# Ten small memsets in place of seven between two indirect writes

## The chip, the cores and the metric

One core of a Trainium2 chip runs the whole program in one launch. The metric is the device time of that launch in microseconds (us), the median of several executions; smaller is better. Before the change three executions took 780.31, 781.12 and 782.70 us, so the median is 781.12 us.

## The reference, cut to what matters

The program is sliding-window attention followed by a mixture of experts that drops no token (float32 throughout). Attention has 8 batches, 8 heads, 576 positions and a head size of 64; heads 0 to 3 look at the last 32 positions, heads 4 to 7 at every fourth of the last 128. The attention output becomes 4,608 token rows of 512 numbers. Each token goes to the one of 8 experts with the largest logit:

```python
scores = np.where(masks, SCALE * q @ k.T, -1e9)
attn   = softmax(scores)              # rows of 576
x      = (attn @ v) as (4608, 512)
logits = x @ w_gate                   # (4608, 8)
e      = argmax(logits, axis=1); gate = softmax(logits)[e]
for each expert: y = relu(x_e @ w1[e]) @ w2[e]    # 512 -> 1024 -> 512
out    = gate[:, None] * y            # back in token order
```

## The kernel before, in words

**Attention.** The 8 batches are cut into 32 units of work, four per batch. A unit goes through the engines in a fixed chain: scores on PE (line 595), masking and the row minimum on DVE (lines 611, 623), nine exponentials on ACT (line 629), the reciprocal of the sums on DVE (lines 640, 642), the normalisation on POOL (line 646, called the norm below), transposes on PE (line 657), their copies on ACT or DVE (line 878) and the product with V on PE (line 676). A ring of three buffers, `e`, holds units between masking and transposes.

**Routing.** After a batch's four units, `route` computes its logits, counts on DVE how many tokens each expert has so far, and writes the batch's 576 rows into a DRAM table called `bucket`, sorted by expert. It does so with five indirect DMAs issued by POOL (`to_bucket`, line 493). After the batches 1, 2, 4 and 7 DVE also computes tables of slots: a slot is 128 rows of one expert. The last route adds two indirect writes of blank rows.

**Experts.** A slot's rows are fetched from `bucket` by SP (`fetch_x`, lines 1379 and 1384), its weights by SP (line 1401), DVE transposes the rows (line 1407), PE does the two layers (lines 1415 and 1431), ACT applies relu and the gate, and POOL scatters the 128 result rows to their tokens by an indirect DMA (line 1456). Thirty such slots and fourteen short ones of 32 rows (lines 1518 to 1545, `own` and `toq` in the trace) are in the planned part. Three slots more come behind it under run-time conditions (`rest`). Slots after batch 1 are computed between the attention units of later batches.

**The order of the work.** No order is written by hand. Each piece of work is given to a planner (`Plan.add`) as a step, with its engines, a cost in us, the steps that it comes after, the buffers that it takes and a rank. `Plan.write` then builds the program: again and again it asks of every open step when it could start on each engine (`could`), takes the earliest time found, and of the steps that could start within 0.25 us of it emits the one of lowest rank. The instructions of each engine are emitted in that order and run in it. While PE is planned to be idle before the first slot, `Plan.write` emits filling matmuls (line 714) whose result nobody reads.

**Indirect writes in the plan.** POOL is planned at 1.0 us per indirect write. If the step that POOL did last was an indirect write too, `could` lets the next one start no earlier than `APART` after the end of the last one, and `write` has `pass_time` (line 720) emit `IDLE` memsets of one element per partition to the tile `still` ahead of it. Any other POOL step between two writes, such as a norm, clears that flag, and then there are no memsets. The planner counts one such memset at 0.21 us:

```python
APART = 0.21 * IDLE                                        # line 138
if s.moved and e == "POOL" and self.last_indirect:         # line 200
    at = max(at, self.wrote + self.APART)
if s.moved and e == "POOL" and self.last_indirect and self.APART:   # line 239
    self.idle()
```

Two further planner constants touch this: an indirect write that starts less than `BURST` (1.0 us) after the last one opens a stretch in which other engines' results are planned to be seen late (`seen`, lines 174 to 180).

Of the kernel before, what the change touches and what calls it, by code (L numbers as in the profile page):

```python
# [63 lines left out]
STEP_W = 1.0  # L64
ROUTE = 5.0

IDLE = 7

MOVED = 3.0
MOVED_S = 1.5  # L70
# [47 lines left out]
class Plan:  # L118
# [18 lines left out]

    APART = 0.21 * IDLE

# [189 lines left out]
def kernel(  # L329
# [390 lines left out]
    def pass_time():  # L720
        for _ in range(IDLE):
            nc.gpsimd.memset(still, 0.0)  # L722
# [1115 lines left out]
```

## Time and profile before

| | |
|---|---|
| runs (us) | 780.31, 781.12, 782.70 |
| profiled execution (us) | 781.74 |
| its span, first to last instruction (us) | 780.0 |
| mean granted TensorE clock | 0.991 |
| PE busy | 742.8 us, 95% of the span |
| DVE, ACT, POOL busy | 33%, 34%, 25% |
| memsets of line 722 | 504, in 72 groups of seven |

The rows come from the hardware profiler's record of that one execution. A row of a timeline has its start and its length in us, the engine, the line of the kernel, the operation, what it writes and reads, and how many instructions are merged in it; in brackets stands how long the engine sat idle before it and whose event ended the wait ("issue" is none that the profile shows). A row of a group of instructions has busy time and mean ns of one, and then the idle time ahead of them with its releasers. A row of a table of stretches has the busy time of each engine in that stretch.

### The profile page before, as it was taken

What the parts mean: (1) busy time and instruction counts of PE and PEld (TensorE: products, weight loads), DVE (VectorE), ACT (ScalarE), POOL (GpSimd) and SP (SyncE); (2) the same over time, 40 slices, a digit from 0 to 9 for tenths busy, and PEclk for the clock granted to TensorE, in tenths of its full rate; (3) what the DMA queues carried; (4) which work ended last, traced back from release to release, by engine and by line L of the source; (5) the groups of instructions that cost most, each with busy time, mean ns of one, the idle gap of its engine ahead of it and who ended that gap; (6) DMA issues with size and microseconds to landing.
All of it is one profiled execution on the core that took longest, in us unless ns stands there. A gap on an engine that the chain in (4) does not pass through costs nothing.

```text
span 780.0 us, 21889 instructions
## 1 busy us (share of the span) xinstructions
PE 742.8 (95%) x8406; PEld 562.4 (72%) x8406; DVE 257.6 (33%) x718; ACT 265.2 (34%) x868; POOL 193.5 (25%) x641
## 2 busy tenths in 40 slices
PE   5879989999999999999999999999999999999996
PEld 5768878868787776776776776777776776766664
DVE  7958858678857740710000000000000000000000
ACT  2766756576747754211111111111111111111100
POOL 1314343425253434260100100211221111102101
PEclk9989999999999999999999999999999999999999
DMA  9878775969997979799629684727678166099660
GB/s 274 301 224 272 229 239 137 361 190 323 260 268 178 298 226 350 262 387 323 214 47 314 201 258 100 254 51 250 196 261 299 35 226 261 22 316 351 257 222 30
DMA packets 140399, 180.68 MB, mean 232 GB/s; under 512 B 68764, under 2 KB 90014, under 8 KB 139776
## 3 DMA queue, kind: packets, MB, share of 16 engines
q1 hardware_dynamic: 132864, 159.00, 64.1%
q0 software_dynamic: 6272, 19.43, 6.5%
q8 instruction: 68, 1.11, 0.6%
q10 hardware_dynamic: 1152, 0.78, 0.4%
q14 instruction: 43, 0.35, 0.1%
HBM read 252.03 MB, written 19.95 MB: 349 GB/s over the span
## 4 chain that ended last, share of the span: by engine, by line
PE 80%; issue 8%; DMA 6%; DVE 3%; ACT 2%; POOL 1%; SPq 0%; POOLq 0%; DVEq 0%; ACTq 0%
PE ph L1415 27%; PE py L1431 25%; PE scores L595 6%; PE xo L676 6%; PE weights L657 4%; DMA qT<-in_moe_w_dram 4%; PE py_s L1545 3%; PE ph_s L1518 3%; PE weights L714 3%; PE xrow L939 2%; PE lp L962 1%; DMA raw<-in_k_dram 1%; DMA x<-bucket 1%; PE logits L976 1%; ACT eT L878 1%
## 5 line engine op out<-in xcount | busy, mean ns | idle before, releaser
L1415 PEld LDWEIGHTS ph<-xt,w 128*128 128x128 f32 x2112 | 243.2, 192 | 15.7 <-issue 14.6
L1415 PE MATMUL ph<-xt,w 128*128 128x128 f32 x2112 | 252.5, 277 | 0.0
L1431 PE MATMUL py<-w,h 128*128 128x512 f32 x528 | 236.5, 594 | 0.6 <-ACT h L1426 0.6
L1431 PEld LDWEIGHTS py<-w,h 128*128 128x128 f32 x528 | 96.0, 190 | 101.3 <-issue 100.8
L629 ACT ACTIVATE e<-e,lo 128x96 f32<-128x96 f32 x288 | 103.5, 363 | 19.6 <-DVE lo L623 19.6
L1407 DVE STREAM_TRANSPOSE xt<-x 128x512 f32<-128x512 f32 x30 | 21.3, 711 | 243.7 <-PE ph L1415 240.4
L1456 POOL DMA_INDIRECT out_dram<-y,to x30 | 29.5, 984 | 251.7 <-ACT y L1436 249.2
L646 POOL TENSOR_TENSOR e<-e,rec 128x864 f32<-128x864 f32 x32 | 52.3, 1633 | 141.1 <-DVE rec L642 112.6
L1426 ACT ACTIVATE h<-ph 128x512 f32<-128x512 f32 x63 | 37.6, 597 | 142.6 <-PE ph L1415 141.8
L1436 ACT ACTIVATE y<-py,gt 128x512 f32<-128x512 f32 x30 | 20.6, 687 | 157.8 <-PE py L1431 150.3
L595 PE MATMUL scores<-kT,qT 32*64 32x96 f32 (+1 forms) x2160 | 56.2, 259 | 12.0 <-issue 7.4
L595 PEld LDWEIGHTS scores<-kT,qT 32*64 32x64 f32 (+1 forms) x2160 | 49.1, 139 | 18.5 <-issue 14.3
L722 POOL MEMSET still<- 128x1 f32 x504 | 51.4, 102 | 25.0
L629 ACT ACTIVATION_READ_ACCUMULATOR e<-e,lo 128x1 f32 x288 | 54.4, 189 | 0.0
L493 POOL DMA_INDIRECT bucket<-rows,idx x40 | 39.2, 980 | 60.9 <-issue 16.9
L676 PEld LDWEIGHTS xo<-eT,v 96*64 96x64 f32 x1280 | 40.9, 138 | 12.3 <-issue 4.5
L657 PE MATMUL weights<-cst,e 128*96 128x128 f32 x288 | 45.1, 282 | 4.5 <-ACT eT L878 2.1
L611 DVE SCALAR_TENSOR_TENSOR e<-scores,cst 128x384 f32<-128x384 f32 (+1 forms) x128 | 45.5, 395 | 10.0 <-PE scores L595 9.0
L676 PE MATMUL xo<-eT,v 96*64 96x64 f32 (+1 forms) x1280 | 45.9, 225 | 3.0 <-issue 2.6
L878 ACT COPY eT<-weights 96x384 f32<-96x384 f32 x88 | 39.9, 480 | 22.8 <-PE weights L657 16.1
L657 PEld LDWEIGHTS weights<-cst,e 128*96 128x96 f32 x288 | 30.2, 129 | 17.2 <-issue 6.8
L1511 DVE STREAM_TRANSPOSE own<-own 128x128 f32<-128x128 f32 x14 | 4.3, 304 | 99.3 <-DMA own<-bucket 99.3
(168 smaller groups left out, 566.5 us busy)
## 6 DMA issues: line engine op xcount, KB each, us to landing
w<-in_moe_w_dram SPq DMA_DIRECT2D x66, 2048.0 KB
raw<-in_moe_w_dram SPq DMA_DIRECT2D x42, 1024.0 KB
qT<-in_moe_w_dram SPq DMA_DIRECT2D x28, 512.0 KB
w<-in_moe_w_dram SPq DMA_DIRECT2D x8, 1024.0 KB
raw<-in_q_dram SPq DMA_DIRECT2D x14, 576.0 KB
raw<-in_k_dram SPq DMA_DIRECT2D x14, 576.0 KB
x<-bucket SPq DMA_DIRECT2D x120, 64.0 KB
v<-in_v_dram SPq DMA_DIRECT2D x7, 864.0 KB
```

Source lines behind the costliest of these rows:

```text
L493: nc.gpsimd.indirect_dma_start(out=bucket, out_offset=bass.IndirectOffsetOnAxis(ap=idx, axis=0), in_=rows, in_offset=None, bounds_check=NR ...
L595: nc.tensor.matmul(two[r][QB * half : QB * half + QB, KB * c : KB * c + KB], lhsT=qT[:, QB * n : QB * n + QB], rhs=kt[:, QB * n : QB * n + ...
L611: nc.vector.scalar_tensor_tensor(out=e[p, c0 : c0 + w], in0=sc[r][p, a : a + w], scalar=-SCALE, in1=m[p, a : a + w], op0=OP.mult, op1=OP.add,)
L629: nc.scalar.activation(out=ev[:, c], in_=ev[:, c], func=AF.Exp, bias=lo[:, c : c + 1], scale=-1.0, accum_out=den[:, c : c + 1],)
L646: nc.gpsimd.tensor_tensor(out=ev, in0=ev, in1=rec.unsqueeze(2).broadcast_to([128, NC, KB]), op=OP.mult)
L657: nc.tensor.transpose(tp[0:KB, c], ev[:, 3 * g + c], ident)
L676: nc.tensor.matmul(xo[DH * r : DH * r + DH, g, lo - half_s * g : hi - half_s * g], lhsT=v0[:, hd, n] if ty == 0 else v1[:, n, hd], rhs=eT[ ...
L722: nc.gpsimd.memset(still, 0.0)
L878: copier(e)(S_["eT"][:, 3 * g : 3 * g + 3], S_["w", g][0:KB, 0:3])
L1415: nc.tensor.matmul(ph[:, f % 4], lhsT=w1s[j % 2][:, c, 128 * f : 128 * f + 128], rhs=xt[:, c], start=c == 0, stop=c == 3,)
L1426: nc.scalar.activation(to, ph, AF.Relu)
L1431: nc.tensor.matmul(py, lhsT=h[:, f], rhs=w2s[j % 2][:, f], start=f == 0, stop=f == 7)
```

## The change

One constant changes. `IDLE` enters in two places: in `pass_time`, which emits that many memsets, and in `APART`, which goes from 1.47 to 2.10 us.

```diff
-IDLE = 7
+IDLE = 10
```

## Rows read from the trace of the kernel before

**Rows 1.** The page: span and busy time of the engines.

```profile
span 780.0 us, 21889 instructions
...
PE 742.8 (95%) x8406; PEld 562.4 (72%) x8406; DVE 257.6 (33%) x718; ACT 265.2 (34%) x868; POOL 193.5 (25%) x641
```

**Rows 2.** Table of stretches: start and end, length, busy us of each engine (instructions), granted clock, DMA share, GB/s.

```profile
0.00:72.00 72.00, 56.49 (x1130) 49.85 (x1131) 55.30 (x117) 40.34 (x171) 17.34 (x30) 0.93 0.86 271
72.00:136.50 64.50, 59.21 (x1082) 51.87 (x1083) 49.37 (x139) 43.13 (x162) 25.10 (x56) 1.00 0.68 204
136.50:345.00 208.50, 200.96 (x2757) 157.70 (x2756) 127.35 (x383) 119.01 (x419) 83.19 (x249) 1.00 0.90 279
345.00:720.00 375.00, 373.65 (x3091) 267.42 (x3090) 22.84 (x77) 57.07 (x107) 62.23 (x296) 1.00 0.64 212
720.00:780.00 60.00, 52.45 (x352) 35.58 (x350) 2.69 (x4) 5.66 (x10) 5.60 (x12) 0.97 0.47 175
```

**Rows 3.** Groups of instructions on PE, from 72 to 136.5 us: the filling matmuls. Then one piece of the chain of work that ended last, in which 24 of them follow one another.

```profile
L714 PE MATMUL weights<-idle 128*128 128x128 f32 x130 | 17.6, 280 | 2.4 <-ACT eT L878 1.7 <-DVE eT L878 0.7
...
100.98 2.94 PE weights L714 x24
```

**Rows 4.** Groups of instructions on POOL: the memsets of line 722 from 72 to 345 us, then from 345 to 735 us, and in the latter stretch the scatters of results.

```profile
L722 POOL MEMSET still<- 128x1 f32 x231 | 23.6, 102 | 11.4
...
L722 POOL MEMSET still<- 128x1 f32 x266 | 27.1, 102 | 13.2
L1456 POOL DMA_INDIRECT out_dram<-y,to x25 | 24.5, 980 | 249.2 <-ACT y L1436 248.4 <-issue 0.7
L1456 POOL DMA_INDIRECT out_dram<-own,toq x14 | 13.7, 978 | 61.8 <-ACT own L1556 30.5 <-DVE toq L1562 18.4 <-DMA qT<-in_moe_w_dram 4.8
```

**Rows 5.** Timeline of POOL, around the first two routes.

```profile
70.76 1.05 POOL L722 MEMSET still<- 128x1 f32 x7
72.46 0.99 POOL L493 DMA_INDIRECT bucket<-rows,idx  x1 [0.65 <-issue]
73.43 1.07 POOL L722 MEMSET still<- 128x1 f32 x7
75.15 0.98 POOL L493 DMA_INDIRECT bucket<-rows,idx  x1 [0.65 <-issue]
...
78.84 1.65 POOL L646 TENSOR_TENSOR e<-e,rec 128x864 f32<-128x864 f32 x1
...
101.49 1.01 POOL L493 DMA_INDIRECT bucket<-rows,idx  x1 [8.97 <-DVE avail L1182]
...
110.55 1.65 POOL L646 TENSOR_TENSOR e<-e,rec 128x864 f32<-128x864 f32 x1
112.36 0.93 POOL L493 DMA_INDIRECT bucket<-rows,idx  x1 [0.17 <-issue]
```

**Rows 6.** Timeline of PE in the same stretch, and of DVE for the reciprocal that the norm at 110.55 us needs.

```profile
84.51 0.86 PE L657 MATMUL weights<-cst,e 128*96 128x128 f32 x6
...
114.32 0.86 PE L657 MATMUL weights<-cst,e 128*96 128x128 f32 x6
...
105.36 0.22 DVE L642 RECIPROCAL rec<-den 128x9 f32<-128x9 f32 x1
```

**Rows 7.** Timeline of POOL: norms that follow writes of the third (152.30 us), fourth and sixth routes; then of PE, the transposes behind three of them.

```profile
152.30 1.63 POOL L646 TENSOR_TENSOR e<-e,rec 128x864 f32<-128x864 f32 x1 [5.55 <-DVE rec L642]
...
183.22 1.63 POOL L646 TENSOR_TENSOR e<-e,rec 128x864 f32<-128x864 f32 x1 [0.43 <-issue]
...
189.35 1.63 POOL L646 TENSOR_TENSOR e<-e,rec 128x864 f32<-128x864 f32 x1 [0.71 <-DVE rec L642]
...
258.32 1.65 POOL L646 TENSOR_TENSOR e<-e,rec 128x864 f32<-128x864 f32 x1
...
186.72 0.53 PE L657 MATMUL weights<-cst,e 128*96 128x128 f32 x3
...
192.40 0.86 PE L657 MATMUL weights<-cst,e 128*96 128x128 f32 x6
...
262.25 0.86 PE L657 MATMUL weights<-cst,e 128*96 128x128 f32 x6
```

**Rows 8.** Timeline of SP's queue, DMA issues around the first slots' rows.

```profile
119.57 8.60 SPq L429 DMA_DIRECT2D v<-in_v_dram  x13
129.29 1.90 SPq L1379 DMA_DIRECT2D x<-bucket  x4
...
135.02 0.37 SPq L379 DMA_DIRECT2D raw<-in_q_dram  x1
...
137.26 1.12 SPq L1401 DMA_DIRECT2D w<-in_moe_w_dram  x2
```

**Rows 9.** Timelines: a norm on POOL; then three short operations of DVE, of which the first starts inside that norm, the second while POOL does nothing, and the third beside the memsets of the last row.

```profile
132.13 1.63 POOL L646 TENSOR_TENSOR e<-e,rec 128x864 f32<-128x864 f32 x1 [4.91 <-DVE rec L642]
...
132.80 0.99 DVE L1029 TENSOR_SCALAR gate<-gate 128x5 f32<-128x5 f32 x1
...
95.46 0.17 DVE L1029 TENSOR_SCALAR gate<-gate 128x5 f32<-128x5 f32 x1
...
105.17 0.15 DVE L640 TENSOR_SCALAR den<-den 128x9 f32<-128x9 f32 x1
...
105.17 1.06 POOL L722 MEMSET still<- 128x1 f32 x7
```

## The prediction

> **What bounds the kernel now.** I read the page's busy times first, then the table of stretches, then POOL's timeline with the norms and writes, and last PE's and SP's timelines at the places that POOL feeds. PE is busy for 95% of the span and POOL for 25% [rows 1]. The table shows where PE is not the bound. From 345 to 720 us it idles 375.00 - 373.65 = 1.4 us, from 136.5 to 345 us 7.5 us, from 72 to 136.5 us 5.3 us [rows 2]. In that last stretch much of its work is filler: 130 matmuls of line 714. Twenty-four of them in a row take 2.94 us, 0.1225 us each, so 130 take about 15.9 us [rows 3]. So from 72 us on PE has 15.9 + 5.3 = 21 us without useful work before the first slot, and 9 us in the 584 us after it. Before 72 us nothing can change: the first memsets come at 70.76 us [rows 5], and up to its first pair of writes the planner decides on the same numbers.
>
> **What three more memsets cost POOL.** From one write to the next it is 75.15 - 72.46 = 2.69 us: the write 0.99, seven memsets 1.07, and 0.65 without an event [rows 5]. The memsets start (1.05 - 0.10) / 6 = 0.158 us apart (0.10 is their mean length [rows 4]), so three more take 0.475 us, and the period becomes 3.17 us. Seven and ten are not both in the trace, so I bound it: 3 x 0.10 = 0.30 if only the busy time counts, 3 x (2.69 - 0.99) / 7 = 0.73 if all of the pause grows with the count. I take 0.475, nearest to the row. There are 504 / 7 = 72 pauses: 33 from 72 to 345 us, 38 behind it [rows 4], one at 70.76 us. If none vanishes, POOL gets 72 x 0.475 = 34 us more, of which 34 x 0.475 = 16 us lie where attention still runs.
>
> **Who waits for POOL, in the order of now.** I shift POOL's work and look for the next reader.
>
> - *Norms behind writes.* The norm at 78.84 us has three pauses before it: 1.43 us later it ends at 81.9 instead of 80.5, and PE's next transposes begin at 84.51 [rows 5, 6]. Cover 4.0 us. The norm at 110.55 us, three pauses again, ends at 113.6 instead of 112.2; the transposes are at 114.32 [rows 5, 6]. Cover 2.1, 0.7 left. In the third route four pauses (1.9 us) meet 5.55 us of idle time before the next norm. In the fourth, two pauses less 0.43 us of idle put the norm of 183.22 us 0.5 us later (PE at 186.72); with the next pause the norm of 189.35 us moves by 0.5 to end at 191.5 (PE at 192.40). In the sixth, two pauses put the norm of 258.32 us 0.95 us later, to end at 260.9 (PE at 262.25) [rows 7]. None reaches PE, so the sum is 0.0 us. Without that cover the first two would cost 2.9 us, all five 4.8 us.
> - *Rows in `bucket`.* The second route's last write ends at 113.3 us, 1.43 us later at 114.7; SP asks for the first slot's rows at 129.29 us, behind 13 loads of V [rows 5, 8]. Cost 0, cover 14 us.
> - *Behind 345 us* a pause runs as soon as the scatter ahead of it is issued. The 25 scatters of slots have 249.2 us of idle time ahead of them, some 10 us each, nearly all of it for their result [rows 4], against 0.475 us. The last pauses before the end lie alike. Cost 0.
> - *DVE.* The Trainium skill ("SBUF — State Buffer", Who interferes with whom) speaks against the change here; the trace first. A DVE operation of 0.17 us took 0.99 us when it began inside a norm, and ended with it (132.80 + 0.99 = 133.79, the norm 132.13 + 1.63 = 133.76). One that began beside the memsets took 0.15 us [rows 9]. So norms hold DVE up and memsets do not, as far as these rows go. The page says that GpSimd and some DVE operations hold one shared pair of ports as an exclusive lock; by that rule more memsets would stop DVE more often. For the norm the trace agrees (0.99 us); for memsets it shows nothing of it. I take 0, and keep the other as a rival.
>
> The sum with the order of now is 0.0 us: 780.0 us of span and 1.74 us around it, 781.7 us. The runs shown have a median 0.6 us below that execution; I put 781.4 us, between the two.
>
> **The order of the work, whose price no row shows.** `APART` goes from 1.47 to 2.10 us, so the planner's period goes from 1.0 + 1.47 = 2.47 to 3.10 us. Measured is 2.69 now, 3.17 worked out above: its error per pause falls from 0.22 to 0.07 us. With the longer pause a norm fits between two writes more often, which also takes that pause's memsets away. From 72 us on the order can change on every engine. What it can give is bounded by the 21 us before the first slot and the 9 us after it. What it can cost is bounded by norms and row fetches that lose their cover, worked out below. I take 0 as the value, since 0.63 us per pause in the plan is less than the covers of 1.0 to 14 us found, and since behind 136.5 us PE has slots to fill with.
>
> **Rivals.**
>
> - *The plan fits better and PE is served earlier: faster.* For it: the norm at 110.55 us had its input from 105.36 + 0.22 = 105.6 us [rows 6] and stood 5.0 us behind writes, while PE ran 24 fillers from 100.98 us [rows 3]. With a pause of 2.10 us in the plan that norm may go ahead of a write. Against it: one norm earlier is not a whole chain earlier, since DVE and ACT are 77% and 67% busy in that stretch (49.37 and 43.13 of 64.5 us [rows 2]). Price: up to 5.0 us, from 2.4 us counting as a gain; about 778.
> - *A norm is emitted behind one more write: slower.* Place: the first two routes, where PE has no slots to turn to. The norm comes one period and three pauses later, 3.17 + 1.43 = 4.6 us. Less the covers of 4.0 and 2.1 us this leaves 0.6 + 2.5 = 3.1 us, 784.8 us; if the fourth route's norm (cover 192.40 - 190.98 = 1.4 us [rows 7]) falls behind as well, 3.2 more, 788.0. It decides from where a norm's shift passes 2.1 us. For it: in both routes the norm stands only one write from the end of the row. Against it: a longer planned pause favours the norm.
> - *The first slot's rows are asked for later: slower.* In the plan the second route's writes end up to 4 x 0.63 = 2.5 us later. If the fetch falls behind the next group of SP's queue (raw loads from 135.02, weights until 138.4 [rows 8]), it goes from 129.29 to 138.4 us, 9.1 us later. Attention can fill about half of that: 4.6 to 9.1 us, 786 to 791. Against it: 14 us lie between writes and fetch now.
> - *The lock on DVE: slower.* 34 pauses with three more memsets of 0.10 us are 10.2 us; DVE is busy 61% of the stretch behind 136.5 us (127.35 of 208.5 [rows 2]), so at most 6.2 us on DVE, under 788; about 784.5 if half of it shows.
> - *The change does not do what it says.* If the pause did not grow (0.65 us of it are no memsets), nothing would change; this lies in the first case.
>
> **How the numbers follow.** Within 0.3% of the runs' median (2.3 us) is about what a measurement of this kernel cannot tell from no change. Chances: no change 0.45 (its own range 779.0 to 783.4); the better plan 0.26; the norm behind one more write 0.17; the late row fetch 0.08; the lock 0.04. That is faster 0.26, the same 0.45, slower 0.29. The range goes from 776.1, which is 781.7 less the whole 5.0 us and the 0.6 us by which the runs lie below the profile, to 787.0, which leaves out most of the late fetch and the double norm.
>
> **What would show it.** Right: groups of ten memsets of about 1.53 us and a period of 3.17 us between writes; 345 to 720 us with PE at 373 to 374 us again; PE idle plus filler from 72 to 136.5 us still near 21 us; the first slot's matmuls (line 1415) near 136.5 us. The better plan would show fewer fillers than 130 and an earlier first slot. The rivals on the other side would show transposes of line 657 that wait for the norm, or the first fetch of rows behind the raw loads, or short DVE operations stretched beside memsets. The prediction is wrong if PE's useful work ends at the same pace but the tail moves, or if the order behind 136.5 us opens waits for weights, which I price at nothing since PE stands at 99.6% from 345 us on.

## The result and the profile after

The changed kernel is slower. Over eight runs of each its median is 786.62 us and that of the kernel before 781.91 us; the ratio is 1.0062 with an interval of 1.0035 to 1.0089. Every ratio here is taken over fast runs alone (a run over 1.5% above the fastest of its kernel does not count), so it need not be the quotient of two medians. The profiled execution of the changed kernel took 786.73 us, with a span of 785.0 us. That lies inside the range of 776.1 to 787.0 us, but the likeliest case, no change, did not come.

The page of the changed kernel, against [rows 1]: the number of records, and busy time of the engines.

```profile
span 785.0 us, 22098 instructions
...
PE 748.1 (95%) x8410; PEld 565.0 (72%) x8410; DVE 259.7 (33%) x719; ACT 263.3 (34%) x867; POOL 213.5 (27%) x847
```

POOL has 20.0 us more busy time. There are 710 memsets now, in 71 groups of ten, which is 206 more of 0.10 us, or 20.6 us. PE is busy 5.3 us longer although it does only four matmuls more (all of them fillers), and that is the first hint: the same matmuls take longer when the granted clock falls, as rows below show.

The table of stretches of the changed kernel, columns as in [rows 2].

```profile
72.00:136.50 64.50, 60.58 (x1126) 53.06 (x1124) 50.56 (x138) 41.93 (x160) 27.30 (x77) 1.00 0.68 204
136.50:345.00 208.50, 200.82 (x2750) 157.34 (x2749) 130.86 (x390) 118.30 (x419) 86.27 (x302) 0.98 0.89 268
345.00:720.00 375.00, 372.80 (x3071) 265.42 (x3070) 22.03 (x76) 56.34 (x106) 77.27 (x422) 1.00 0.63 213
```

Of these, only the middle stretch has another granted clock than before, 0.98 for 1.00. (Ahead of 72 us it is 0.88 for 0.93 [rows 2]; the last section comes back to that.) The long one behind it idles 2.2 us, as against 1.4 us: nothing happens there. To see where the middle loses, I asked for the waits of PE from 136 to 345 us in the changed kernel (engine, line, waited for: us in total, times, longest).

```profile
PE xrow L939 <- DVE rows L950: 4.3, 1, 4.3
PE lp L962 <- issue: 0.7, 1, 0.7
```

One wait stands out. PE's timeline shows what stands around it:

```profile
170.01 1.02 PE L1431 MATMUL py<-w,h 128*128 128x512 f32 x2
175.34 1.97 PE L939 MATMUL xrow<-cst,xT 128*128 128x128 f32 x8 [4.31 <-DVE rows L950]
177.10 0.84 PE L657 MATMUL weights<-cst,e 128*96 128x128 f32 x3
177.74 1.65 PE L1431 MATMUL py<-w,h 128*128 128x512 f32 x2
179.23 0.60 PE L939 MATMUL xrow<-cst,xT 128*128 128x128 f32 x4
```

The same pair of `py` matmuls takes 1.02 us ahead of the wait and 1.65 us behind it. The table of stretches of the changed kernel in steps of 5 us gives the reason (last three columns: granted clock, DMA share, GB/s):

```profile
165.00:170.00 5.00, 5.00 (x104) 4.28 (x97) 0.42 (x3) 1.45 (x3) 1.63 (x1) 1.00 1.06 335
170.00:175.00 5.00, 1.03 (x4) 0.20 (x2) 3.75 (x4) 2.04 (x11) 0.00 (x0) 0.72 0.78 235
175.00:180.00 5.00, 4.66 (x18) 3.56 (x19) 4.59 (x20) 2.57 (x11) 1.21 (x1) 0.60 0.52 112
180.00:185.00 5.00, 4.16 (x58) 3.17 (x57) 2.40 (x9) 2.53 (x5) 2.44 (x12) 1.00 0.43 114
```

PE waits for DVE's copy of the routed rows (`rows`, line 950), since the buffer that its next transposes fill must be emptied first. So I went to DVE's timeline in the changed kernel:

```profile
165.27 0.21 DVE L642 RECIPROCAL rec<-den 128x9 f32<-128x9 f32 x1
171.22 0.71 DVE L1407 STREAM_TRANSPOSE xt<-x 128x512 f32<-128x512 f32 x1 [5.74 <-DMA x<-bucket]
171.86 1.01 DVE L623 TENSOR_REDUCE lo<-e 128x9 f32<-128x864 f32 x1
172.79 1.24 DVE L538 STREAM_TRANSPOSE qT<-raw 128x576 f32<-128x576 f32 x1
174.06 1.23 DVE L950 COPY rows<-xrow 128x1024 f32<-128x1024 f32 x1
```

DVE stands for 5.74 us at the transpose of the third slot's rows, which have not landed. Behind that instruction, in DVE's fixed order, are three others, and the third is the copy that PE needs. In SP's queue and in the chain of work that ended last, the fetch of these rows looks so:

```profile
159.92 0.39 SPq L1401 DMA_DIRECT2D w<-in_moe_w_dram  x1
161.68 1.93 SPq L1379 DMA_DIRECT2D x<-bucket  x4
...
163.30 7.80 DMA x<-bucket
```

The rows take 7.80 us from the start of their last issue, while the planner adds 2.5 us to a transfer for its landing (`LANDS`, line 124). A load of 2 MB of weights was issued just ahead of them on the same queue.

The kernel before has the same trap, but milder. Rows of it at this place: the fetch on SP's queue, its landing in the chain of work, then DVE, ACT and PE.

```profile
159.42 1.93 SPq L1379 DMA_DIRECT2D x<-bucket  x4
...
161.03 6.49 DMA x<-bucket
...
167.65 0.71 DVE L1407 STREAM_TRANSPOSE xt<-x 128x512 f32<-128x512 f32 x1 [3.27 <-DMA x<-bucket]
...
166.63 1.01 ACT L950 COPY rows<-xrow 128x1024 f32<-128x1024 f32 x1 [0.98 <-PE xrow L939]
...
171.47 0.51 PE L657 MATMUL weights<-cst,e 128*96 128x128 f32 x3 [1.76 <-DVE dl L989]
```

There ACT made the copy, as soon as PE had filled the buffer, while DVE stood for 3.27 us. What PE waited for was the choice of experts (`dl`, line 989), which stands behind the transpose on DVE: 1.76 us, at a granted clock of 1.00 from 170 to 180 us.

### The profile page after: what moved, and what is told of

It reads as the page before. It is cut to its first block, busy times and chain, and to the rows that moved or that the text cites. A ratio compares the mean times of both kernels' runs of the same rounds, so it can differ in the third digit from the quotient of the medians.

```text
span 785.0 us, 22098 instructions
## 1 busy us (share of the span) xinstructions
PE 748.1 (95%) x8410; PEld 565.0 (72%) x8410; DVE 259.7 (33%) x719; ACT 263.3 (34%) x867; POOL 213.5 (27%) x847
## 4 chain that ended last, share of the span: by engine, by line
PE 80%; issue 8%; DMA 5%; DVE 4%; ACT 2%; SPq 1%; POOL 1%; POOLq 0%; DVEq 0%; ACTq 0%
PE ph L1415 27%; PE py L1431 24%; PE scores L595 6%; PE xo L676 6%; PE weights L657 4%; DMA qT<-in_moe_w_dram 3%; PE py_s L1545 3%; PE ph_s L1518 3%; PE weights L714 3%; PE xrow L939 2%; PE lp L962 1%; DMA x<-bucket 1%; PE logits L976 1%; DVE kT L549 1%; DMA raw<-in_q_dram 1%
## 5 line engine op out<-in xcount | busy, mean ns | idle before, releaser
L722 POOL MEMSET still<- 128x1 f32 x710 | 71.6, 101 | 36.9
L1436 ACT ACTIVATE y<-py,gt 128x512 f32<-128x512 f32 x30 | 20.6, 687 | 147.2 <-PE py L1431 145.6
L878 ACT COPY eT<-weights 96x384 f32<-96x384 f32 x89 | 40.5, 484 | 20.6 <-PE weights L657 15.3
L623 DVE TENSOR_REDUCE lo<-e 128x9 f32<-128x864 f32 x32 | 33.1, 1035 | 0.7
```

Source lines behind the costliest of these rows:

```text
L878: copier(e)(S_["eT"][:, 3 * g : 3 * g + 3], S_["w", g][0:KB, 0:3])
```

## The experiments

Two explanations stood at first: the longer planned pause put the instructions of some engines into another order, and that order costs the time; or the memsets themselves cost it, on POOL or by holding up DVE. As the constant feeds both, the first two kernels take them apart.

**Ten memsets in the order of before.** `APART` stays at 1.47 us.

```diff
-        for _ in range(IDLE):
+        for _ in range(10):
```

> Ten memsets are emitted, but the planner keeps 1.47 us as its pause, so every engine runs the order of the kernel before. Theory A (the new order costs the time, the memsets do not): as before, ratio 0.998 to 1.002, no norm and no row fetch that PE waits for, period between writes 3.16 us. Theory B (the longer pause itself costs): ratio 1.004 to 1.008, as in the changed kernel.

Measured: 1.0007, interval 0.9973 to 1.0041 (medians of all runs 777.85 us, and 780.56 us for the kernel before beside it). The memsets cost nothing that can be measured. Its page, its POOL timeline and its waits of PE from 165 to 190 us:

```profile
PE 741.3 (95%) x8406; PEld 563.0 (72%) x8406; DVE 257.9 (33%) x718; ACT 265.9 (34%) x868; POOL 215.3 (28%) x857
...
76.00 0.98 POOL L493 DMA_INDIRECT bucket<-rows,idx  x1 [0.65 <-issue]
76.97 1.53 POOL L722 MEMSET still<- 128x1 f32 x10
79.15 0.98 POOL L493 DMA_INDIRECT bucket<-rows,idx  x1 [0.65 <-issue]
...
PE weights L657 <- DVE dl L989: 4.7, 1, 4.7
```

The period is 79.15 - 76.00 = 3.15 us, POOL works 21.8 us more than before, and DVE 257.9 us for 257.6 us. The last row is a warning: in this execution the old order's wait was 4.7 us, and yet its span was only 779.6 us. More on that below.

**Seven memsets in the order of after.** `IDLE` is 10 for the planner, seven are emitted.

```diff
-        for _ in range(IDLE):
+        for _ in range(7):
```

> Seven memsets are emitted, but the planner counts 2.10 us as its pause, so every engine runs the order of the changed kernel. Theory A: slow as the changed kernel, ratio 1.004 to 1.008, with PE idle for about 4 us near 171 us behind the DVE transpose that waits for a slot's rows. Theory B: as before, ratio 0.998 to 1.002.

Measured: 1.0088, interval 1.0052 to 1.0124. The whole loss is there without one added memset, so it is the order's. Waits of PE in this kernel:

```profile
PE xrow L939 <- DVE rows L950: 4.3, 1, 4.3
```

**The changed kernel again**, unedited, beside these two.

> The changed kernel once more. Both theories: ratio near 1.006. It also says whether the 2.5 us by which its first indirect write came later than in the kernel before (72.2 against 69.7 us), in a part whose order is the same in both, comes again: if it is chance, the first write moves by a us or more from run to run; if it belongs to the changed kernel, it stays near 72.2 us.

Measured: 1.0068, interval 1.0031 to 1.0104. Its longest wait of PE is the same one:

```profile
PE xrow L939 <- DVE rows L950: 5.3, 1, 5.3
```

**The third slot's transpose behind the copy.** The changed kernel, in which DVE alone gets another order: the transpose of the third slot's rows (`j == 2`, as slots are counted from 0) is held back and emitted behind the copy of the first rows of the fourth route (`b == 3`).

```diff
-    after_route = {}
+    after_route, held = {}, {}
...
+            if (b, g) == (3, 0):
+                held.pop("xt")()
...
+            cross = lambda e, j=j, D=D: D.update(xt=across(j))
+            if j == 2:
+                cross = lambda e, now=cross: held.update(xt=lambda: now(e))
-            xt = add("DVE", 0.72, lambda e, j=j, D=D: D.update(xt=across(j)), after=[xl],
+            xt = add("DVE", 0.72, cross, after=[xl],
```

> The changed kernel with one DVE instruction moved back by three places: the transpose of the third slot's rows stands behind the row minimum, the turning of a q tile and the copy of routed rows that PE waits for, in place of ahead of them; nothing else in any engine's order changes. Theory A with this wait as the cause: PE's 4.3 us wait near 171 us goes, some of it comes back at the fourth route's rank because the same transpose now waits ahead of that; 2 to 4 us faster than the changed kernel, ratio 1.001 to 1.004. If the loss is spread over many small places or lies ahead of 72 us: ratio stays at 1.005 to 1.007.

Measured: 0.9992, interval 0.995 to 1.0034, 0.0076 below the changed kernel of the same comparison, or some 5.9 us; the two intervals only just meet. DVE's timeline in this kernel, in which line 1407 has become 1409 and line 1431 has become 1433:

```profile
164.11 1.23 DVE L950 COPY rows<-xrow 128x1024 f32<-128x1024 f32 x1 [1.27 <-PE xrow L939]
...
166.73 0.71 DVE L1409 STREAM_TRANSPOSE xt<-x 128x512 f32<-128x512 f32 x1 [1.39 <-DMA x<-bucket]
```

DVE still waits for the rows, but the copy is done by then. PE's longest wait from 165 to 190 us is 0.6 us. One DVE instruction, moved past a few others, gives the loss back. The gain was larger than the 2 to 4 us expected.

**The same in the kernel before**, with the transpose held back until the fourth route's experts are chosen (`if b == 3: held.pop("xt")()` at the end of that step).

> The kernel before (seven memsets, old order) with the third slot's transpose on DVE moved back behind the fourth route's choice of experts; nothing else moves. Theory A (in either order DVE stands at this transpose until the rows land, and PE waits for what is queued behind it): the wait of PE near 171 us (1.8 us in the first profile of the kernel before, 4.7 us in the one with ten memsets in its order) goes, ratio 0.993 to 0.998. Rival (only the new order puts something behind it that PE needs at once): ratio 0.998 to 1.002.

Measured: 0.9969, interval 0.9949 to 0.999. Its trace has no wait of PE for DVE from 165 to 190 us. The kernel before loses some 0.3%, or 2.4 us (0.8 to 4.0 by the interval), at this place.

**The changed kernel with the transpose behind the copy and the choice.** (The text below calls the third slot's transpose behind the copy "e5".)

> The changed kernel with the third slot's transpose moved back behind the copy of routed rows and behind the choice of experts too, five DVE operations further than in e5. Theory A: the same gain as there, and the 0.5 us that PE still waited for the choice goes as well: ratio 0.994 to 1.001, PE's wait at 171 us under 0.5 us. Rival (the gain there was chance): ratio 1.004 to 1.008.

Measured: 0.9958, interval 0.9927 to 0.999, and no wait of PE from 165 to 190 us. It is faster than the kernel before, and its interval lies wholly below that of the changed kernel. Its PE has the same order as the changed kernel's, so the two timelines can be set side by side. Rows of this one, which answer to those of the changed kernel from 170.01 us on:

```profile
167.68 1.02 PE L1433 MATMUL py<-w,h 128*128 128x512 f32 x2
168.54 1.04 PE L939 MATMUL xrow<-cst,xT 128*128 128x128 f32 x8
169.42 0.49 PE L657 MATMUL weights<-cst,e 128*96 128x128 f32 x3
169.74 1.02 PE L1433 MATMUL py<-w,h 128*128 128x512 f32 x2
170.69 0.66 PE L939 MATMUL xrow<-cst,xT 128*128 128x128 f32 x4
```

| start of the same PE work (us) | changed | this one | later by |
|---|---|---|---|
| `py` ahead of the wait | 170.01 | 167.68 | 2.33 |
| `xrow` x8, behind the wait | 175.34 | 168.54 | 6.80 |
| `xrow` x4 | 179.23 | 170.69 | 8.54 |
| `weights` | 184.57 | 175.07 | 9.50 |
| `py`, the next batch | 210.04 | 198.97 | 11.07 |

The first 2.33 us are there from the first write on (72.23 us as against 69.85). The wait adds 4.47 us, the low clock 1.74 us, and small waits behind the late work another 2.5 us, together 8.7 us. The ratios, which come from two comparisons with the kernel before, say 1.0062 - 0.9958 = 0.0104, some 8 us.

**Twelve memsets**, planned and emitted (`IDLE = 12`): a third order, to see whether the cost follows the length of the pause or an accident of the order.

> IDLE = 12: twelve memsets and a planned pause of 2.52 us, so a third order. Theory A (what costs is which order comes out, by the waits that it happens to hold): the ratio follows from this order's own waits of PE between 136 and 200 us, and need not lie above the changed kernel's; 0.995 to 1.006 if PE waits less than 3 us there. Theory B' (a longer planned pause costs in proportion, 0.62% for three steps): ratio 1.008 to 1.013.

Measured: 1.009, interval 1.0062 to 1.0118. The wait at 171 us is not there; from 165 to 190 us PE waits at most 1.0 us at a time. This order loses elsewhere: its fillers (line 714, by what they write) number 296, as against 266 in the kernel before.

```profile
L714 PE MATMUL weights<-idle 128*128 128x128 f32 x238 | 34.0, 287 | 3.7 <-ACT eT L878 2.2 <-DVE eT L878 1.4
L714 PE MATMUL unread<-idle 128*128 128x128 f32 x54 | 9.7, 353 | 3.5 <-POOL idle L710 3.5
L714 PE MATMUL rank<-idle 128*128 128x128 f32 x4 | 0.7, 300 | 0.3 <-DVE pick L1018 0.3
```

Thirty more of 0.1225 us [rows 3] are 3.7 us by estimate, and its first slot begins at 141.8 us, although its first write comes at 70.32 us, nearly as early as before. A second loss lies behind it. Two rows of its table of stretches, and the same matmuls on PE ahead of them and inside them:

```profile
190.00:195.00 5.00, 4.57 (x111) 3.98 (x113) 1.94 (x4) 4.51 (x22) 2.77 (x20) 0.73 1.01 379
195.00:200.00 5.00, 5.00 (x36) 4.83 (x33) 4.73 (x10) 1.36 (x2) 4.12 (x9) 0.59 0.85 270
...
144.10 2.94 PE L1415 MATMUL ph<-xt,w 128*128 128x128 f32 x24
...
196.69 4.02 PE L1415 MATMUL ph<-xt,w 128*128 128x128 f32 x24
```

Here the granted clock fell to 0.73 and 0.59 with no wait of PE above 1.0 us since 165 us. The ratio lies where Theory B' put it. Theory A's 0.995 to 1.006 was tied to less than 3 us of waits from 136 to 200 us, and this order has 4.5 us (the kernel before 4.0 us). So the number fits a cost that grows with the planned pause, and the trace shows other losses than with ten; that the fillers and the clock make up the 7 us was not tried by itself, and this experiment does not decide between the two theories.

**The kernel before, run once more**, for its wait in another execution.

> The kernel before once more, for a second profile. Both theories: the same waits; it says by how much the first indirect write (69.7 us) and PE's wait near 171 us (1.8 us) move from one execution to the next.

Measured: 781.27 us. Its wait of PE:

```profile
PE weights L657 <- DVE dl L989: 1.4, 1, 1.4
```

With the order of before this wait was 1.8, 1.4 and, with ten memsets, 4.7 us; with the order of after, 4.3, 4.3 and 5.3 us. The old order also gets part of its loss back. Set side by side on PE with the kernel of the same order and the transpose held back, the one with ten memsets runs 2.42 us ahead at 162 us, 3.55 us behind at 179 us, and 0.48 us behind at 242 us: 6.0 us lost and 3.1 us regained in between. The changed kernel regains nothing: by 210 us it has lost 8.7 us. This may be how a wait of 4.7 us could go with a ratio of 1.0007.

## Why the prediction was wrong in its likeliest case

- *What three more memsets cost POOL: right.* Predicted was a period of 3.17 us; measured is 78.61 - 75.45 = 3.16 us. POOL's timeline of the changed kernel, which answers to [rows 5]:

```profile
75.45 0.99 POOL L493 DMA_INDIRECT bucket<-rows,idx  x1 [0.65 <-issue]
76.42 1.54 POOL L722 MEMSET still<- 128x1 f32 x10
78.61 0.98 POOL L493 DMA_INDIRECT bucket<-rows,idx  x1 [0.65 <-issue]
81.74 1.63 POOL L646 TENSOR_TENSOR e<-e,rec 128x864 f32<-128x864 f32 x1 [2.16 <-DVE e L611]
...
104.26 1.02 POOL L493 DMA_INDIRECT bucket<-rows,idx  x1 [8.74 <-DVE avail L1182]
...
111.60 1.65 POOL L646 TENSOR_TENSOR e<-e,rec 128x864 f32<-128x864 f32 x1
```

The 0.65 us without an event did not grow with the count, so the upper bound of 0.73 us per pause falls.

- *Who waits for POOL, in the order of now: right, and shown.* The sum of 0.0 us was for an order that stays, and the kernel with ten memsets in that order took 1.0007; no wait of PE from 136.5 to 345 us in its trace is for a norm. The lock on DVE is out with it: DVE's busy time there was 257.9 us for 257.6 us. The Trainium skill's rule of a shared lock ("SBUF — State Buffer", Who interferes with whom) shows in these traces for norms alone [rows 9].
- *Behind 345 us: right.* PE is busy 372.80 of 375.00 us there, just under the 373 to 374 us forecast.
- *The better plan.* Its first half came: the norm now stands behind three writes in both of the first routes, where it stood behind four, at 81.74 and 111.60 us. Its gain did not. In the second route the norm began 7.3 us behind the first write (104.26 us), for 9.1 us before; in the first, where it waited 2.16 us for DVE, 9.5 us behind it (72.23 us), for 9.1 us before. From 72 to 136.5 us there are again 130 fillers that write `weights`. The first slot began at 141.2 us, and at 137.1 to 141.4 us in the other runs with this order on PE, while their first writes came from 69.85 to 74.08 us, so a good part of that difference is there before the orders part. Counted from the first write it is 66.9 to 69.0 us with this order, and 64.4 to 66.8 us with the order of before.
- *The step that failed is "The order of the work, whose price no row shows", which I took at 0.* I checked the plan's change of 0.63 us per pause against covers of POOL's own products, norms and rows in `bucket`. The cost came on an engine that has no part in the pauses. The new order made DVE, no longer ACT, copy the rows, and put that copy behind the transpose of the third slot's rows, which land late in either order. Its price was 8 us in the new order where it had been 2.4 us in the old; apart from this place the two orders are alike, 0.9969 and 0.9958 with the transpose held back. The difference of those two ratios, 0.9 us, is within their intervals; 8.1 - 2.4 - 0.9 = 4.8 us is the 0.62% again, as it must be, and no further check.
- *My reason for the 0 was also wrong.* I wrote that behind 136.5 us PE has slots to fill with. PE runs one fixed order, so while it stood for 4.3 us at the transposes (line 939), the matmuls of experts and attention behind them could not go first. The prediction's own last sentence named this, an order behind 136.5 us that "opens waits for weights", and priced it by the calm of the stretch from 345 us on, where DVE has little to do.
- *The rival nearest to it* was the third, rows of a slot that come late. There it was the first slot, asked for later by SP; what came was the third slot, asked for no later when counted from the first write (161.68 - 72.23 = 89.4 us, before 159.42 - 69.72 = 89.7 us) and landing 1.3 us later from its issue (7.80 for 6.49 us). The harm was done by what stood behind it on DVE. That its price of 4.6 to 9.1 us was of the right size is luck, as it was worked out for another fetch.
- *That the time lies inside the range is luck as well.* The upper end of 787.0 us came from a norm behind one more write and a late first fetch, and neither happened.

What stays open: why these rows need 6.5 to 7.9 us from the last issue was not tried (the weights ahead of them on the queue are argued, not shown); and why one constant sent the copy to DVE is the planner's arithmetic, which no trace shows.

## What to carry to other kernels

A constant that a planner reads is two changes, what is emitted and what is reordered; run each by itself before blaming either. In the trace, look for an engine that stands at a load, and read what is queued behind it: if the bound engine needs one of those instructions, move the one that waits for the load behind them, which here was worth 0.3% to 1% for one instruction. Covers have to be checked on all engines that the planner may reorder, not on the one whose cost was changed.

## What the runs showed that I had not expected

- PE's wait of 4.3 us cost more than itself. The granted clock, 1.00 up to 170 us, was 0.60 from 175 to 180 us and 1.00 again from 180 us; in the second run of the changed kernel, after a wait of 5.3 us, it was 0.50 from 175 to 180 us, the lower of the two levels (1.2 GHz). Eight `xrow` transposes took 1.97 us for 1.04 us. Waits of 1.4 and 1.8 us at the same place in the kernel before left it at 1.00; after the 4.7 us with ten memsets it was 0.84 from 170 to 175 us and 0.82 from 175 to 180 us. No long wait came before it in another run: with twelve memsets the clock fell to 0.59 behind a stretch from 185 to 190 us in which PE was busy 4.07 of 5 us and waited at most 0.9 us at a time. The row of the second run of the changed kernel:

```profile
175.00:180.00 5.00, 4.12 (x14) 2.95 (x15) 4.59 (x20) 2.97 (x13) 0.67 (x1) 0.50 0.50 112
```

- The start of the first write, up to which all these kernels do the same, wandered between 69.6 and 74.1 us from one execution to the next. It went with the granted clock ahead of it: in the traces with 0.88 to 0.94 from 40 to 68 us the first write came at 69.6 to 70.5 us, in those with 0.79 to 0.83 at 72.2 to 74.1 us. Differences of 2 to 4 us between two traces at 72 us say nothing here of the change.
